# Fused attention and two feed-forward layers on one core: the first batch's last query tile moved behind the third unit, the third unit's gate products put ahead, values products tied behind later scores

## The chip, the core and the metric

The program runs on one core of a Trainium2 chip. The metric is the device time of one execution in microseconds (us). Engines by their short names: PE multiplies matrices (PEld is its weight load), DVE is the vector engine, ACT the scalar engine, POOL is GpSimd, and SP issues most of the DMAs. Every engine takes its instructions in the order in which the built program lists them.

## What is computed

```python
# attention: q, k, v (4, 8, 576, 64), block-causal mask with blocks of 64
scores = where(block_i >= block_j, q @ k.T / 8, -1e9)
x = softmax(scores) @ v                    # (4, 8, 576, 64) -> 2304 tokens x 512
# first layer: RMS norm, gate and values of width 1536
xn = x / sqrt(mean(x * x) + 1e-6) * rms_g
x = (silu(xn @ w_gate) * (xn @ w_val)) @ w_out
# second layer: one of 8 experts for every token
expert = argmax(cosine(x, expert_emb) / tau)
out = gate_w * (relu(x @ w1[expert]) @ w2[expert])
```

Products run in two half-precision parts (high and low), so that each takes three matrix products: high by high, high by low, low by high.

## The kernel before

**Tiles and units.** A batch has 576 tokens: four query tiles of 128 rows (t = 0 to 3) and a last one of 64 rows (t = 4). `TILES` lists the pairs (b, t) in the order in which attention is computed: for every batch tiles 0 and 1, then 2 and 3, then 4. The first layer works on nine units of 256 tokens: unit 0 is tiles (0,0) and (0,1), unit 1 is (0,2) and (0,3), unit 2 is (1,0) and (1,1), and so on; the four last tiles (b,4) together are unit 8. `need[u]` is the number of attention groups that must be done before unit u can start. A group is a few heads of one tile: all eight for t = 0, four for t = 1, two else.

**A group of attention.** `attend_a` loads and prepares the inputs that are due (`att_load`, `prep`: keys and queries are split and turned, for tiles from the fifth on by DMA transposes that SP issues), then computes the scores (`att_qk`, into two PSUM tiles `sc`, of which there are two), their maxima (`att_max`, on DVE and ACT), the exponentials (`att_exp`, ACT) and the split into high and low parts `ph` and `pl` (`att_split`; for t = 4 `pl` is made on DVE, L412, else on POOL, L417), which from the twelfth group on are turned by two DMA transposes into `pth` and `ptl`. `att_pv` multiplies these by the values into `av`. After a tile's last head, `fin_all` normalises it: x, jk, the power on POOL (L494), the scaling on DVE (L499), hl (ACT L505 and POOL L511), and a DMA transpose into the unit's columns `xT` (L513). `x` and `hl` have one buffer each.

**A unit of the first layer.** `gate_mm(u, s)` makes 24 gate and 24 values products for one of six slices of the width; `gate_t`, `gate_a` and `gate_b` make the two halves of `hT[s]` from them. `out_mm(u, j, s)` adds the slice to the output of token half j (six products a slice and half), and `out_ev` takes that output from PSUM to the tile `R` (one buffer), squares it in place (ACT L580, after which the PSUM tile `o` is free) and turns it (`x2T`).

**The order.** Three stages matter. In the list `pair`, four gates of unit 0 run between the groups of its neighbours; then 14 steps interleave the slices of unit 0's output with the gates of unit 1. Behind each step as many groups are attended as `want` says, up to `need[2] + AHEAD` at the end, and two weight steps (`w_step`: load, decode on DVE L189 to L193, split on ACT L203, L204 and POOL L205) follow. `tc.cur_priority` and a scheduler decide the final order there. From unit 2 on the PE order is written out by hand: `piece(u, s, n)` gives six pieces a slice (two of output of unit u - 1, then four of gates of unit u), and `due` says behind which piece the scores and the values products of each group come. Lines of the kernel after the change are two to twenty higher than before (L567 of the output products becomes L571, L530 becomes L535, L505 becomes L510, L411 and L412 become L413 and L414).

The table of inputs, `xt` (three buffers for the units' columns), `kv` (six for keys, seven for values) and the constants AHEAD = 3, LATER = 7 are the numbers that the change touches or relies on.

Of the kernel before, what the change touches and what calls it, by code (L numbers as in the profile page):

```python
# [18 lines left out]
P = 128  # L19
# [12 lines left out]
def attention_moe_moe(ctx: ExitStack, tc: tile.TileContext, q, k, v, w_gate, w_val, w_out, rms_g, emb, tau, w1, w2, out):  # L32
# [40 lines left out]
    xt_p = p1.enter_context(tc.tile_pool(name="xt", bufs=3))  # L73
    ps_s = p1.enter_context(tc.tile_pool(name="ps_s", bufs=2, space=PSUM))
    ps_a = p1.enter_context(tc.tile_pool(name="ps_a", bufs=1, space=PSUM))
    kv_p = p1.enter_context(tc.tile_pool(name="kv", bufs=6))
# [11 lines left out]
    AHEAD, NW0, NW1, NW2, WLAG, NLAG, LOADS, PREPS, PRI, EVERY, LATER = 3, 4, 2, 2, 2, 1, 3, 1, 300, 4.8, 7  # L88
# [205 lines left out]
    def prep_v(b, t):  # L294
        n = rows_of(t)
        vv = kv_p.tile([P, H, 2 * D], F16, tag="vT", name="vT", bufs=7)
        vT[b, t] = vv
        src = nat.pop(("v", b, t))[:n]
        nc.scalar.activation(out=vv[:n, :, 0:D], in_=src, func=ACTF.Copy, scale=QS)
        nc.gpsimd.tensor_tensor(out=vv[:n, :, D:2 * D], in0=src, in1=vv[:n, :, 0:D], op=ALU.subtract)  # L300
# [5 lines left out]
    sc_t = {}  # L306

    def att_qk(b, t, heads):
        scs = [ps_s.tile([P, 512], F32, tag="sc", name="sc") for _ in range(2)]
        sc_t[b, t, heads[0]] = scs  # L310
        if t < NTT - 1:
            keys = P * (t + 1)
            hpb = 512 // keys
            for bk, sc in enumerate(scs):
                for j, h in enumerate(heads[bk * hpb:(bk + 1) * hpb]):
# [5 lines left out]
                nc.tensor.matmul(  # L321
                    out=sc[:, 0:hpb * keys].rearrange("p (j k) -> p j k", k=keys)[:, :, keys - 64:keys],
                    lhsT=mask_l, rhs=mask_r[:, 0:64 * hpb].rearrange("p (j k) -> p j k", k=64),
                    start=False, stop=True, skip_group_check=True)
        else:
            half = S // 2
            for hf, sc in enumerate(scs):
# [5 lines left out]
                for c in range(2):  # L333
                    for n, (kt, a, z) in enumerate(pieces):
                        for j, h in enumerate(heads):
                            nc.tensor.matmul(out=sc[64 * j:64 * j + 64, a - hf * half:z - hf * half], lhsT=q_of(b, t, h, c),
                                             rhs=kT[b, kt][:, h, a - kt * P:z - kt * P],
                                             start=(c == 0 and n == 0), stop=(c == 1), skip_group_check=True)
# [95 lines left out]
    def att_pv(b, t, heads):  # L434
# [7 lines left out]
        for j, h in enumerate(heads):  # L442
            o = a[0][0:n, h, :]
            for kb in range(nkb):
# [6 lines left out]
                for i, (x, w) in enumerate(((lh, vv[0:kn, h, 0:D]), (lh, vv[0:kn, h, D:2 * D]), (ll, vv[0:kn, h, 0:D]))):  # L451
                    first = a[1] is None
                    mm = nc.tensor.matmul(out=o, lhsT=x, rhs=w, start=first, stop=(h == H - 1 and kb == nkb - 1 and i == 2), skip_group_check=True)  # L453
                    if first:
# [102 lines left out]
    fl = {}  # L557
# [313 lines left out]
    for u, (b, z) in enumerate(HALVES):  # L871
        TILES += [(b, 2 * z), (b, 2 * z + 1)]
        spot[b, 2 * z], spot[b, 2 * z + 1] = (u, 0), (u, P)
        if z:
            TILES.append((b, NTT - 1))
            spot[b, NTT - 1] = (NU - 1, b * (UNIT // B))
    groups = []
# [133 lines left out]
    n0, n1 = need[1], need[2] + AHEAD  # L1011
    for i, (kind, u, s, want) in enumerate(pair):
# [3 lines left out]
        while state["g"] < want:  # L1016
            attend()
            w_step(NW1 if i < 4 else 0)
# [14 lines left out]
    def piece(u, s, n):  # L1033
        if n < 2:
            out_mm(u - 1, n, s)
            if n and s == NFP - 1:
                out_ev(u - 1, 0)
                out_ev(u - 1, 1)
        else:
# [3 lines left out]
            if n == 5:  # L1043
                gate_a(u, s)
                gate_b(u, s)
# [3 lines left out]
                if s == 1:  # L1049
                    for f in (route_c, route_p, route_d):  # L1050
                        f(u - 2, [0, 1])

    with tc.manual_schedule(engines={ENG.PE}):
        for i in range(pieces + 1):
# [5 lines left out]
            if i < pieces:  # L1060
                piece(2 + i // (6 * NFP), i // 6 % NFP, i % 6)
# [198 lines left out]
```

## Time and profile before

| what | value |
|---|---|
| time, median of 3 runs | 867.86 us |
| time, lowest and highest | 864.2 and 868.99 us |
| the profiled execution's own time | 866.45 us |
| its span | 864.6 us |
| mean granted TensorE clock | 0.968 |
| busy: PE, DVE, ACT, POOL | 793.1, 464.2, 451.2, 355.3 us |

The span runs from the first to the last instruction; the time has 1.85 us more around it. The three runs lie within 0.6% of each other. PE is busy for 92% of the span, so the table alone says little: what the change can win is read from the stretch in which its order differs.

### The profile page before, as it was taken

To read this page: it belongs to the slowest core of one execution; us is meant where nothing else is said; L and a number is where in the kernel's file an instruction comes from. 1 tells how busy PE (TensorE), PEld (TensorE's weight loads), DVE (VectorE), ACT (ScalarE), POOL (GpSimd) and SP (SyncE) were. 2 spreads that over 40 slices of the span, in tenths; PEclk is the share of its full clock that TensorE was granted. 3 is DMA by queue.
4 is the path that set the end of the run, shared out by engine and by line. 5 is a ranking of instruction groups with operands and counts; after the bars stand their busy time and mean duration, and the time that the engine had idled before them with its cause. 6 is when DMAs were issued, how large, how long until landed. Compare 5 with 4: busy or idle time off the path is not lost. (4 is left out here: it accounts for less than half of the span.)

```text
span 864.6 us, 21945 instructions
## 1 busy us (share of the span) xinstructions
PE 793.1 (92%) x8590; PEld 602.7 (70%) x8590; DVE 464.2 (54%) x984; ACT 451.2 (52%) x929; POOL 355.3 (41%) x362
## 2 busy tenths in 40 slices
PE   3769799879999999989999999999899999999994
PEld 2669577657767777767777777767676777777771
DVE  6799988735255636245636254134573175471352
ACT  6888777755555656555656452122521274462352
POOL 5555556764552656542656521223314121202110
PEclk8789989999999999999999999999999999999998
DMA  8474799986688686587686351022784399897760
GB/s 243 145 193 140 165 244 232 158 155 107 111 162 156 105 135 124 112 157 152 114 135 119 77 106 32 7 49 50 218 247 113 77 300 302 216 316 197 185 154 22
DMA packets 291326, 130.39 MB, mean 151 GB/s; under 512 B 247613, under 2 KB 276456, under 8 KB 291211
## 3 DMA queue, kind: packets, MB, share of 16 engines
q1 hardware_dynamic: 283338, 112.28, 60.1%
q0 software_dynamic: 4080, 10.56, 4.3%
q10 hardware_dynamic: 3792, 6.03, 2.1%
q8 instruction: 70, 1.15, 0.6%
q14 instruction: 46, 0.37, 0.1%
HBM read 129.30 MB, written 10.25 MB: 161 GB/s over the span
## 5 line engine op out<-in xcount | busy, mean ns | idle before, releaser
L530 PE MATMUL g<-xT,wg 128*128 128x256 f16 x1296 | 157.0, 276 | 2.5 <-DMA xT<-hl 2.5
L567 PE MATMUL o<-wo,hT 128*128 128x512 f16 x648 | 153.5, 384 | 3.8 <-ACT o L580 3.8
L530 PE MATMUL v<-xT,wv 128*128 128x256 f16 x1296 | 156.7, 275 | 0.0
L530 PEld LDWEIGHTS <-wg 128*128 128x128 f16 x1296 | 125.9, 99 | 24.8 <-issue 1.8
L530 PEld LDWEIGHTS <-wv 128*128 128x128 f16 x1296 | 123.9, 98 | 15.4
L763 PE MATMUL h<-xt,whi 128*128 128x128 f16 x1280 | 109.8, 219 | 0.8 <-DVE xt L1073 0.8
L763 PE MATMUL h<-xt,wlo 128*128 128x128 f16 x640 | 108.4, 219 | 0.3 <-DVEq L736 0.3
L567 PEld LDWEIGHTS <-hT 128*128 128x128 f16 x648 | 60.7, 98 | 68.0 <-issue 6.3
L728 DVE SCALAR_TENSOR_TENSOR wlo<-raw,whi 128x1024 f16<-128x1024 f32 x64 | 77.6, 1239 | 46.2 <-ACT whi L727 44.2
L763 PEld LDWEIGHTS <-whi 128*128 128x128 f16 x1280 | 98.9, 98 | 5.0 <-issue 0.9
L787 PE MATMUL o<-whi,hl 128*128 128x512 f16 x320 | 96.4, 383 | 2.3 <-issue 2.3
L555 POOL TENSOR_TENSOR hT<-h,hT 128x512 f16<-128x512 f32 x54 | 63.2, 1170 | 70.3 <-ACT hT L554 68.4
L417 POOL TENSOR_TENSOR pl<-pf,ph 128x512 f16<-128x512 f32 x66 | 69.5, 1073 | 53.7 <-issue 46.7
L787 PEld LDWEIGHTS <-hl 128*128 128x128 f16 x480 | 46.3, 98 | 56.9 <-issue 5.9
L795 POOL DMA_INDIRECT out_dram<-ob,ido x18 | 21.0, 1168 | 151.4 <-ACTq L736 76.1
L727 ACT ACTIVATE whi<-raw 128x1024 f16<-128x1024 f32 x64 | 65.9, 1053 | 31.3 <-DMA raw<-in_moe_w_dram 19.9
L453 PE MATMUL av<-vT,ptl 128*128 128x64 f16 (+2 forms) x480 | 57.5, 198 | 25.5 <-DMA ptl<-pl 15.6
L353 DVE TENSOR_REDUCE nb<-sc 128x1 f32<-128x384 f32 (+3 forms) x88 | 54.0, 635 | 44.7 <-PE sc L321 44.4
L453 PE MATMUL av<-vT,pth 128*128 128x64 f16 (+2 forms) x960 | 65.7, 198 | 7.9 <-DVE c L193 3.5
L453 PEld LDWEIGHTS <-pth 128*128 128x128 f16 (+2 forms) x960 | 53.8, 105 | 19.3 <-DMA pth<-ph 9.1
L453 PEld LDWEIGHTS <-ptl 128*128 128x128 f16 (+2 forms) x480 | 45.9, 105 | 30.6 <-DMA ptl<-pl 18.5
L372 ACT ACTIVATE pf<-sc,nb 128x128 f32<-128x128 f32 (+3 forms) x128 | 65.9, 526 | 2.3 <-ACT nb L354 0.4
(230 smaller groups left out, 1300.4 us busy)
## 6 DMA issues: line engine op xcount, KB each, us to landing
raw<-in_moe_w_dram SPq DMA_DIRECT2D x172, 512.0 KB
st<-in_moe_w_out_dram SPq DMA_DIRECT2D x12, 512.0 KB
st<-in_moe_w_gate_dram SPq DMA_DIRECT2D x11, 512.0 KB
st<-in_moe_w_val_dram SPq DMA_DIRECT2D x11, 512.0 KB
x2s<-R ACTq DMA_DIRECT2D x18, 256.0 KB
nat<-in_k_dram SPq DMA_DIRECT2D x16, 256.0 KB
nat<-in_q_dram SPq DMA_DIRECT2D x16, 256.0 KB
nat<-in_v_dram SPq DMA_DIRECT2D x16, 256.0 KB
```

Of the source, the lines that this page charges most:

```text
L353: nc.vector.tensor_reduce(out=nb[:, z], in_=sc[:, 0:hpb * keys].rearrange("p (j k) -> p j k", k=keys), axis=AX.X, op=ALU.max)
L372: nc.scalar.activation(out=pf[:, j * keys:(j + 1) * keys], in_=scs[j // hpb][:, (j % hpb) * keys:(j % hpb + 1) * keys], func=ACTF.Exp, sca ...
L417: nc.gpsimd.tensor_tensor(out=pl[:, z:y], in0=pf[:, z:y], in1=ph[:, z:y], op=ALU.subtract)
L453: mm = nc.tensor.matmul(out=o, lhsT=x, rhs=w, start=first, stop=(h == H - 1 and kb == nkb - 1 and i == 2), skip_group_check=True)
L530: mm = nc.tensor.matmul(out=o[:, j, :], lhsT=w[cw][:, kt, f * P:(f + 1) * P], rhs=x[:, cx * KD + kt, :], start=(n == 0), stop=(n == 3 * KD ...
L555: nc.gpsimd.tensor_tensor(out=hT[1][fp], in0=h, in1=hT[0][fp], op=ALU.subtract)
L567: mm = nc.tensor.matmul(out=o, lhsT=hT[ch][f // 2][:, f % 2, j * P:(j + 1) * P], rhs=wo[cw][:, f, :], start=(f == 0 and n == 0), stop=(f = ...
L727: hi = nc.scalar.activation(out=whi[l][c], in_=raw[l][c], func=ACTF.Copy, scale=ES)
L728: lo = nc.vector.scalar_tensor_tensor(out=wlo[l][c], in0=raw[l][c], scalar=ES, in1=whi[l][c], op0=ALU.mult, op1=ALU.subtract)
L763: mm = nc.tensor.matmul(out=h[:, f, :], lhsT=w[:, kt, :], rhs=x[:, cx * KD + kt, :], start=(n == 0), stop=(n == 3 * KD - 1))
L787: nc.tensor.matmul(out=o, lhsT=x[:, cx, kt, :], rhs=w, start=(n == 0), stop=(n == 3 * K2 - 1))
L795: nc.gpsimd.indirect_dma_start(out=out, out_offset=bass.IndirectOffsetOnAxis(ap=(ido if ids is None else ids)[:, i:i + 1], axis=0), in_=ob ...
```

## The change

It has five parts. (1) Tile (0,4) is taken from the fifth place of `TILES` and put behind (1,1), so that its four groups come after those of unit 2's two tiles; `need[2]` falls from 18 to 14 and AHEAD rises from 3 to 7, which leaves the number of groups attended in the `pair` stage at 21. (2) In that stage, from the fifth step on, the values products of a group are written two groups later, and their first one is tied on PE behind the last score product written before it; the two that are left over go to the first two places of `due`. (3) For unit 2's first slice the four gate pieces come before the two output pieces of unit 1, and `gate_b` of that slice comes behind the output. (4) The units' columns have two buffers instead of three. (5) Keys have seven buffers instead of six, values eight instead of seven.

```diff
-    xt_p = p1.enter_context(tc.tile_pool(name="xt", bufs=3))
+    xt_p = p1.enter_context(tc.tile_pool(name="xt", bufs=2))
...
-    kv_p = p1.enter_context(tc.tile_pool(name="kv", bufs=6))
+    kv_p = p1.enter_context(tc.tile_pool(name="kv", bufs=7))
...
-    AHEAD, NW0, NW1, NW2, WLAG, NLAG, LOADS, PREPS, PRI, EVERY, LATER = 3, 4, 2, 2, 2, 1, 3, 1, 300, 4.8, 7
+    AHEAD, NW0, NW1, NW2, WLAG, NLAG, LOADS, PREPS, PRI, EVERY, LATER = 7, 4, 2, 2, 2, 1, 3, 1, 300, 4.8, 7
...
-        vv = kv_p.tile([P, H, 2 * D], F16, tag="vT", name="vT", bufs=7)
+        vv = kv_p.tile([P, H, 2 * D], F16, tag="vT", name="vT", bufs=8)
...
-    def att_pv(b, t, heads):
+    def att_pv(b, t, heads, behind=None):
...
+                    if behind:
+                        tc.add_manual_dep(mm.ins, behind, NOSYNC, reason="those scores go first")
+                        behind = None
...
+    TILES.insert(6, TILES.pop(4))
...
+    pend = []
     for i, (kind, u, s, want) in enumerate(pair):
...
         while state["g"] < want:
-            attend()
-            w_step(NW1 if i < 4 else 0)
+            if i < 4:
+                attend()
+                w_step(NW1)
+            else:
+                attend_a()
+                if len(pend) > 1:
+                    att_pv(*pend.pop(0), behind=fl['qk'])
+                pend.append(groups[state["g"] - 1])
...
     def piece(u, s, n):
         if n < 2:
             out_mm(u - 1, n, s)
+            if n and (u, s) == (2, 0):
+                gate_b(u, s)
...
-                gate_b(u, s)
+                if (u, s) != (2, 0):
+                    gate_b(u, s)
...
+    for g, a in zip((first - 2, first - 1), sorted(due)):
+        due[a].append(("pv", g))
...
-                piece(2 + i // (6 * NFP), i // 6 % NFP, i % 6)
+                piece(2 + i // (6 * NFP), i // 6 % NFP, i % 6 if i > 5 else (2, 3, 4, 5, 0, 1)[i])
```

In `att_qk` the score products also store their name in `fl['qk']`, and `fl = {}` moves up.

How the order of the built program moves is shown at three places. Names: `sc` are scores of a group, `kT` and `qT` turned keys and queries, `av` a tile's output, `o` the first layer's output of a token half, `g` and `v` gate and values products; a number behind a name tells buffers apart.

First place: PE, where the output of unit 0's first slices ends and unit 1's first gate (on xT_1181) begins. Before, with scores of tile (0,4) (sc_1878, sc_1992) and its values products (av_1764):

```order
L567 MATMUL o_1710<-wo1_194,hT0_1_196 128x512
...
L336 MATMUL sc_1878<-kT_242,qT_1595 64x128
...
L453 MATMUL av_1764<-vT_276,pth_1758 64x64
...
L336 MATMUL sc_1992<-kT_242,qT_1597 64x128
...
L453 MATMUL av_1764<-vT_276,ptl_1761 64x64
...
L567 MATMUL o_1703<-wo0_193,hT0_2_197 128x512
...
L530 MATMUL g_1815<-xT_1181,wg0_189 128x256
```

After, with scores of (1,1) in two groups (sc_1865, sc_1952), values products of (1,0) (av_1990), scores of (0,4) (sc_2180) and values products of (1,1) (av_2227):

```order
L571 MATMUL o_1716<-wo0_193,hT1_1_202 128x512
...
L320 MATMUL sc_1865<-kT_1734,qT_1738 128x128
...
L320 MATMUL sc_1952<-kT_1734,qT_1740 128x128
...
L455 MATMUL av_1990<-vT_1605,pth_1784 128x64
...
L571 MATMUL o_1709<-wo0_193,hT0_2_197 128x512
...
L338 MATMUL sc_2180<-kT_242,qT_1945 64x128
...
L455 MATMUL av_2227<-vT_1605,pth_1900 128x64
...
L535 MATMUL g_1808<-xT_1181,wg0_189 128x256
```

Four groups of scores now stand ahead of unit 1's first gate where three of (0,4) stood, and the first values products stand behind two later groups' scores.

Second place: ACT, up to the copy `hl` of tile (0,3), from which the second half of xT_1181 is turned. Before (`pf` are exponentials, `ph` high parts, `c` and the `w` names are weights):

```order
L378 ACTIVATE pf_1748,sums_1747<-sc_1717,nb_1743 128x288
L378 ACTIVATE pf_1748,sums_1747<-sc_1718,nb_1743 128x288
L203 ACTIVATE wv0_191<-c_1285 128x4x128
L204 ACTIVATE c_1285<-c_1285 128x512
L488 ACTIVATE jk_1674,fin_1670<-x_1669 128x512
L203 ACTIVATE wg0_189<-c_1425 128x4x128
L411 ACTIVATE ph_1754<-pf_1748,sums_1747 128x576
L204 ACTIVATE c_1425<-c_1425 128x512
L505 ACTIVATE hl_1679<-x_1669 128x512
```

After:

```order
L416 ACTIVATE ph_1779<-pf_1770 128x1024
L493 ACTIVATE jk_1680,fin_1676<-x_1675 128x512
L251 ACTIVATE qd_1937<-nat_1725 64x8x2x64
L204 ACTIVATE c_1425<-c_1425 128x512
L356 ACTIVATE nb_1885<-nb_1885 128x4
L203 ACTIVATE wv0_191<-c_1435 128x4x128
L374 ACTIVATE pf_1890,sums_1889<-sc_1865,nb_1885 128x256 x2
L374 ACTIVATE pf_1890,sums_1889<-sc_1866,nb_1885 128x256 x2
L204 ACTIVATE c_1435<-c_1435 128x512
L416 ACTIVATE ph_1895<-pf_1890 128x1024
L510 ACTIVATE hl_1685<-x_1675 128x512
```

Between the last group of (0,3) and this copy stood one group of (0,4); now a whole tile (1,0), the first group of (1,1) and the preparation of (0,4) stand there.

Third place: PE, where the output of unit 0 ends and that of unit 1 begins. Before (o_1710 is unit 0, o_3119 and o_3126 unit 1, g_3181 is unit 2's first gate on xT_2463):

```order
L567 MATMUL o_1710<-wo0_193,hT1_5_206 128x512
L530 MATMUL g_3060<-xT_1181,wg0_189 128x256
L567 MATMUL o_3119<-wo0_193,hT0_0_195 128x512
L530 MATMUL v_3085<-xT_1181,wv0_191 128x256
L567 MATMUL o_3126<-wo0_193,hT0_0_195 128x512
L530 MATMUL g_3181<-xT_2463,wg0_189 128x256
```

After (o_1716 is unit 0, o_3238 unit 1, g_3083 and v_3176 unit 2's first gate on xT_2028):

```order
L571 MATMUL o_1716<-wo0_193,hT1_5_206 128x512
L535 MATMUL g_3024<-xT_1181,wg0_189 128x256
L535 MATMUL v_3049<-xT_1181,wv0_191 128x256
L535 MATMUL g_3083<-xT_2028,wg0_189 128x256
L535 MATMUL v_3176<-xT_2028,wv0_191 128x256
L571 MATMUL o_3238<-wo0_193,hT0_0_195 128x512
```

Unit 1's output now waits for the PSUM tile of unit 0's behind 96 gate products. Outside these places the PE order is the same, row for row, up to the last groups of tile (0,3) and again from the second slice of unit 1's output on.

## Rows read from the trace of the kernel before

**Rows 1.** The page: busy time of each engine over the span.

```profile
PE 793.1 (92%) x8590; PEld 602.7 (70%) x8590; DVE 464.2 (54%) x984; ACT 451.2 (52%) x929; POOL 355.3 (41%) x362
```

**Rows 2.** Stretches: length, busy PE, PEld, DVE, ACT, POOL (instructions), granted clock, DMA share, GB/s.

```profile
93.10:111.83 18.73, 13.39 (x163) 8.27 (x162) 18.50 (x48) 13.79 (x33) 8.27 (x8) 0.84 0.68 184
111.83:204.30 92.47, 83.79 (x875) 65.80 (x874) 58.60 (x104) 62.04 (x145) 59.96 (x58) 0.92 0.98 189
```

**Rows 3.** Timeline of PE, where it stood idle: start, us, operation, [idle before, releaser].

```profile
105.75 0.32 PE L453 MATMUL av<-vT,pth 128*64 128x64 f16 x2 [3.48 <-DVE c L193]
...
111.83 4.77 PE L530 MATMUL g<-xT,wg 128*128 128x256 f16 x24 [1.07 <-DMA xT<-hl]
...
156.72 0.23 PE L453 MATMUL av<-vT,pth 128*128 128x64 f16 x2 [2.53 <-DMA pth<-ph]
...
192.63 2.72 PE L567 MATMUL o<-wo,hT 128*128 128x512 f16 x6 [3.09 <-ACT o L580]
```

**Rows 4.** Timeline of PE, at full clock: what products take from start to start.

```profile
119.43 0.74 PE L336 MATMUL sc<-kT,qT 128*64 128x128 f16 x24
...
123.15 0.22 PE L453 MATMUL av<-vT,ptl 128*64 128x64 f16 x1
...
124.67 0.94 PE L530 MATMUL v<-xT,wv 128*128 128x256 f16 x7
...
143.90 3.19 PE L567 MATMUL o<-wo,hT 128*128 128x512 f16 x14
146.93 2.78 PE L530 MATMUL g<-xT,wg 128*128 128x256 f16 x24
...
161.37 2.78 PE L530 MATMUL g<-xT,wg 128*128 128x256 f16 x24
163.99 2.56 PE L530 MATMUL v<-xT,wv 128*128 128x256 f16 x22
166.39 0.50 PE L318 MATMUL sc<-kT,qT 128*128 128x128 f16 x6
...
167.12 0.38 PE L530 MATMUL v<-xT,wv 128*128 128x256 f16 x2
...
172.92 0.22 PE L453 MATMUL av<-vT,pth 128*128 128x64 f16 x2
...
173.62 0.22 PE L453 MATMUL av<-vT,pth 128*128 128x64 f16 x2
```

**Rows 5.** Timeline of ACT: prices, and the copies of tile (0,3).

```profile
83.14 0.62 ACT L505 ACTIVATE hl<-x 128x512 f16<-128x512 f32 x1
83.66 0.62 ACT L203 ACTIVATE wo<-c 128x512 f16<-128x512 f32 x1
...
93.80 0.60 ACT L397 ACTIVATE pth<-pT 128x512 f16<-128x512 f32 x1
...
103.40 0.63 ACT L505 ACTIVATE hl<-x 128x512 f16<-128x512 f32 x1 [0.31 <-DVE x L499]
...
140.47 0.36 ACT L372 ACTIVATE pf<-sc,nb 128x128 f32<-128x128 f32 x1
...
145.61 1.08 ACT L414 ACTIVATE ph<-pf 128x1024 f16<-128x1024 f32 x1
...
157.94 0.47 ACT L372 ACTIVATE pf<-sc,nb 128x256 f32<-128x256 f32 x1
```

**Rows 6.** Timeline of SP: the transpose of tile (0,3) into xT.

```profile
106.98 1.23 SPq L513 DMA_TRANSPOSE xT<-hl  x1
```

**Rows 7.** Timeline of POOL: first and last of six instructions without a gap.

```profile
147.88 2.27 POOL L417 TENSOR_TENSOR pl<-pf,ph 128x512 f16<-128x512 f32 x2
...
153.44 1.16 POOL L555 TENSOR_TENSOR hT<-h,hT 128x512 f16<-128x512 f32 x1
```

**Rows 8.** Timeline of DVE: the scaling of a tile, twice.

```profile
102.62 0.74 DVE L499 SCALAR_TENSOR_TENSOR x<-x,fin,g_b 128x512 f32<-128x512 f32 x1
...
148.38 6.76 DVE L499 SCALAR_TENSOR_TENSOR x<-x,fin,g_b 64x512 f32<-64x512 f32 x1
```

More of the change, by code (lines that the diff above doesn't have):

```diff
@@ L306, in attention_moe_moe @@
     sc_t = {}
+    fl = {}
     def att_qk(b, t, heads):
@@ L320, in att_qk @@
                                              skip_group_check=True)
-                nc.tensor.matmul(
+                fl['qk'] = nc.tensor.matmul(
                     out=sc[:, 0:hpb * keys].rearrange("p (j k) -> p j k", k=keys)[:, :, keys - 64:keys],
                     lhsT=mask_l, rhs=mask_r[:, 0:64 * hpb].rearrange("p (j k) -> p j k", k=64),
-                    start=False, stop=True, skip_group_check=True)
+                    start=False, stop=True, skip_group_check=True).ins.name
         else:
@@ L335, in att_qk @@
                         for j, h in enumerate(heads):
-                            nc.tensor.matmul(out=sc[64 * j:64 * j + 64, a - hf * half:z - hf * half], lhsT=q_of(b, t, h, c),
+                            fl['qk'] = nc.tensor.matmul(out=sc[64 * j:64 * j + 64, a - hf * half:z - hf * half], lhsT=q_of(b, t, h, c),
                                              rhs=kT[b, kt][:, h, a - kt * P:z - kt * P],
-                                             start=(c == 0 and n == 0), stop=(c == 1), skip_group_check=True)
+                                             start=(c == 0 and n == 0), stop=(c == 1), skip_group_check=True).ins.name
     pt_t = {}
@@ L555, in gate_b @@
         nc.gpsimd.tensor_tensor(out=hT[1][fp], in0=h, in1=hT[0][fp], op=ALU.subtract)
-    fl = {}
     x2T = {}
```

## The prediction, made before the changed kernel was run

> **What bounds the kernel now.** I read the page first: PE is busy 793.1 of 864.6 us [rows 1], so a change that adds no work can win only from PE's idle time and from stretches at the lower clock. The order shows where to look: PE's products differ only between the last group of tile (0,3), at 93.1 us, and the second slice of unit 1's output, at 204.3 us. The second view is therefore the table of stretches [rows 2]. From 93.10 to 204.30, 111.2 us, PE is busy 97.2 and idle 14.0, and the granted clock is 0.84 and 0.92. The third view, PE's timeline, names the idle places: 3.48 us before the first values product of (0,4), 1.07 before unit 1's first gate, 2.53 before those of (1,0), 3.09 where unit 1's output waits for ACT to free the PSUM tile of unit 0's [rows 3]. After such a pause PE runs at the lower clock: 24 gate products took 4.77 us at 111.83 and 2.78 at 146.93 [rows 3, 4].
>
> The products of this stretch can be priced at full clock [rows 4]. Gates and values: 2.62 us for 24, 0.109 each. Output: 3.03 for 14, 0.216 each. Scores: 0.74 a group of (0,4), else 0.73 for 14, 0.052 each. Values products: 0.70 for 24, 0.029 each, and for (0,4) 1.52 for 29, 0.052 each. The stretch holds 432 gates (47.2), 84 output products (18.2), four score groups of (0,4) and 128 other score products (3.0 + 6.7), 150 values products and 120 of (0,4) (4.4 + 6.3), and about 1.5 of small ones: 87.3 us. So 24 us is the most that any order could win, 14 of idle time and 10 of low clock.
>
> **The change part by part.**
>
> *Tile (0,4) later, tied values products: the first half.* The stretch to unit 1's first gate is one in which DVE is busy 18.50 of 18.73 us [rows 2]. The change takes the four groups of (0,4), whose low parts DVE makes, out of it and puts in (1,0) and (1,1), whose low parts POOL makes. DVE is relieved; ACT, in order and filled, becomes the engine that ends last. Its list tells when unit 1's second half of columns can be ready. The first `pth` copy of (0,3)'s last group started at 93.80 [rows 5]; now one 1024-wide copy stands ahead of it, 1.08 long and about 0.98 from start to start, so 94.8. From there to the copy `hl` of (0,3) stand 15 instructions of 512 columns, 0.52 from start to start (7.8), two more 1024-wide ones and the third, `ph` of (1,1) (2.9), eight exponentials of 128 columns at 0.36 (2.9), four of 256 at 0.47 (1.9) and two small ones (0.4) [rows 5]: 15.9 us, so `hl` starts at 110.7 instead of 103.40. From there to the gate it took 8.43 us before, with the transpose issued at 106.98 [rows 3, 5, 6]. POOL now has the low part of (1,1), 2.27 us [rows 7], ahead of `hl`'s, which begins at 110.7 too and costs 1.65 beyond the copy's own 0.62. So unit 1's first gate starts at 110.7 + 8.4 + 1.6 = 120.7 us instead of 111.83: the first half is 8.9 us **later**. PE will stand idle there, mostly at the first values products of (1,0) (whose transposes cannot be issued before ACT's `ph`) and at the scores behind them, which need one of two `sc` tiles back.
>
> *The second half.* What is left from that gate to the end of the stretch is 432 gates (47.2), 52 output products (11.2), three groups of (0,4) scores (2.2), 74 other score products (3.9), 100 values products (2.9), 120 of (0,4) (6.3), router (0.5): 74.2 us, where it took 92.47. I add 2.0 for the low clock behind the pause, as at 111.83. The waits: every group's values products now stand behind a later group's scores, so that the transposes have a gate's time more; the 2.53 us at 156.72 should go.
>
> *Gates of unit 2 ahead of unit 1's output.* 96 gate products (10.5), scores (0.7) and 18 values products (0.5), 11.7 us, now stand between the last output product of unit 0 and the first of unit 1. Before, the first half of unit 1's output stood right behind, and the second half came 3.09 us too early for its tile [rows 3]. Against the change: both halves of unit 0 now end together, so the second must pass the one tile `R` behind the first, its transpose (about 4.9 us, the 106.98 to 111.83 of [rows 3, 6]) included, and the copies; 11.7 covers that with little to spare, and I leave half a microsecond of the 3.09 in the waits below. The low clock behind that wait (2.72 us for six products, where 0.216 each would be 1.3 [rows 3, 4]) goes too.
>
> *Two buffers for columns.* Unit 2's columns now take the buffer of unit 0, so SP's transpose of (1,0) waits for unit 0's last gate, and everything behind it on SP's list with it: the transposes of (1,2) first. `x` and `hl` have one buffer, so (1,1), then (0,4) follow: a transpose of 4.9 us again and a chain of about as much, against 13.4 us of PE work (66 gates 7.2, 58 values products of (0,4) 3.0, 28 scores 1.5, eight output products 1.7) before PE needs (1,2)'s output tile. I cost it at nothing; if that cover is short it shows as a wait of `av`. More key and value buffers, and the two values groups moved into `due`, cost nothing: no product is added.
>
> *Sum.* For the waits that stay in the second half I take 2.0 us of the 8.7 idle before (92.47 less 83.79 [rows 2]). The stretch ends at 120.7 + 2.0 + 74.2 + 2.0 = 198.9 instead of 204.3. That is 5.4 us less than the profiled execution's own 866.45 (which lies 1.4 below the median of the three runs, 867.86): **861.0 us**. Bounds of the uncertain terms: the gate at 111.83, if ACT's list keeps its old pace, or at 126.7, if the chain is hit by one such block as at 148.38 (below, 6.0 us); waits of 0 to 5 in the second half. That is 850 to 870.
>
> **A rule against it.** At 148.38 DVE's scaling of a tile took 6.76 us, at 102.62 it took 0.74 [rows 8]. In the first case POOL worked through six instructions without a gap from 147.88 to 154.60 and DVE ended half a microsecond after the last [rows 7]; it was held through all six. The change fills POOL's list in just the place where the scaling of (0,3) falls. On the row's price a hit there that nothing hides adds 6.0 us to the sum: 867. The Trainium skill ("SBUF — State Buffer", section "Who interferes with whom") says that a DVE instruction with two SBUF inputs contends with a GpSimd instruction that reads SBUF and that the one that issues first holds the port for the whole instruction; read as one instruction of waiting, 1.16 us at most, its price would make the sum 861 to 862 even with such a hit. The row shows longer.
>
> **Rivals.**
> (a) *The wait only moves.* The first gate starts later still, at 123 to 126, since SP's list puts three weight loads ahead of that transpose, each waiting for DVE to free a buffer. For it: DVE at 99% in the first half. Against it: DVE loses the work of (0,4) there. The second half's gain is then spent: gain -1 to 3.5, 863 to 867, say 865.5.
> (b) *The first half costs nothing.* DVE was its only limit, ACT keeps up, and the gate comes at 112 to 114: gain 12 to 14, 853. Against it: the ACT sum above, which has no idle time in it.
> (c) *Slower: DVE is held by POOL.* POOL's runs in the first half and after hold the scaling of (0,3), (1,0) and (1,1) and the low parts of (0,4) as at 148.38. One hit of 6.0 is mostly hidden behind the ACT chain; two more, in front of DVE's steps on gate products, stop PE, 12.0 less 5.4: 6.6 slower, 873. It decides from about 10 us of holding on. For it: one such row; against it: POOL must have no gap in its run, and at 102.62 the same step took 0.74 [rows 8].
> That the ties are not kept is ruled out by the order, which shows them on PE.
>
> **How the numbers follow.** About 0.5% (4.3 us) can be told from no change. My forecast, a gain of 2 to 9 us, has 0.48 (0.34 beyond 4.3, 0.14 within), (a) 0.20 (all within), (b) 0.18 (beyond), (c) 0.14 (0.12 slower, 0.02 within). Faster 0.52, same 0.36, slower 0.12. The range of 853 to 868.5 leaves out (c) and the best part of (b).
>
> **What would show it.** Right: PE idle by more than before ahead of unit 1's first gate, which starts at about 120; no wait of some 3 us at unit 1's first output; hardly any idle time and a clock of 1.00 from there to the router; everything behind the stretch only shifted. Wrong: the gate before 115 or after 125; a DVE row of several us in the stretch; PE waiting for `av` after unit 0's last gate; a difference behind the second slice of unit 1's output.

## The result, and the profile after

The changed kernel takes 861.4 us (median of 8 runs, 857.1 to 861.92) against 868.08 of 8 runs of the kernel before: ratio 0.9914, 95% interval 0.989 to 0.9938 (the two medians alone give 0.9923). In a second set, on another chip, it was 0.9925 (0.9895 to 0.9954). It is faster by 0.75 to 0.86%, 6.5 to 7.5 us; 861.0 was predicted. The profiled execution took 859.82 us, with a span of 858.0.

The page has the same totals as before [rows 1], to within 6 us:

```profile
PE 787.3 (92%) x8590; PEld 600.6 (70%) x8590; DVE 464.2 (54%) x984; ACT 449.7 (52%) x929; POOL 355.1 (41%) x362
```

The table of stretches (columns as in [rows 2]) is cut at the same three places of the program as there: the last group of tile (0,3), unit 1's first gate, the second slice of unit 1's output.

```profile
92.48:122.58 30.10, 18.10 (x169) 11.29 (x170) 26.14 (x39) 23.29 (x64) 22.03 (x20) 0.79 1.10 228
122.58:201.97 79.39, 76.95 (x869) 61.96 (x868) 53.69 (x121) 51.28 (x113) 44.79 (x44) 1.00 0.78 160
201.97:858.00 656.03, 628.14 (x6804) 470.17 (x6800) 305.97 (x657) 300.30 (x579) 235.59 (x230) 0.99 0.64 142
```

The first part takes 30.10 us where it took 18.73, and PE is busy in it for 18.10 us instead of 13.39. The second takes 79.39 instead of 92.47, at a clock of 1.00 instead of 0.92, with 2.4 us idle instead of 8.7. Little of this is work that changed its place. Counted by kind and priced by [rows 4], an estimate, the first part's products come to about 11.9 us against 10.2 before, so 1.8 us moved ahead of the gate (six more output products are 1.3 of it); the rest of the 4.7 us by which PE is busier there goes with the low clock (0.79; an output product took 441 ns on average, before 398). Over both parts PE idles 14.4 us instead of 14.0 and is busy for 95.05 instead of 97.18: the change put the idle time ahead of the gate, and what is behind it then runs at full clock. So the stretch ends at 201.97 instead of 204.30: 2.33 us, not 5.4. The other 4.27 us of difference in span lie behind it, where the program is the same (before, the last part took 864.60 - 204.30 = 660.30). That needs an explanation, below.

PE's timeline in the first part and at the end of the second (start, us, operation, [idle before, releaser]):

```profile
109.45 0.82 PE L320 MATMUL sc<-kT,qT 128*128 128x128 f16 x8 [4.47 <-ACT pf L374]
112.59 0.23 PE L455 MATMUL av<-vT,ptl 128*128 128x64 f16 x1 [1.00 <-DMA ptl<-pl]
118.07 1.23 PE L338 MATMUL sc<-kT,qT 128*64 128x128 f16 x24 [3.27 <-DMA qT<-qd]
122.50 0.26 PE L455 MATMUL av<-vT,pth 128*128 128x64 f16 x2 [0.53 <-DVE x L484]
122.58 3.16 PE L535 MATMUL g<-xT,wg 128*128 128x256 f16 x24
...
197.69 0.18 PE L612 MATMUL L<-enT,x2T 128*128 128x16 f16 x1 [0.62 <-DMA x2T<-R]
...
197.91 2.75 PE L571 MATMUL o<-wo,hT 128*128 128x512 f16 x12
```

PE idles at scores that wait for an `sc` tile and at the scores of (0,4), whose turned queries are late. The gate itself runs almost at full clock (3.16 us for 24, where [rows 3] show 4.77). Unit 1's output now runs without the 3.09 us wait of [rows 3].

The chain that sets the gate, on ACT, POOL and SP (three timelines):

```profile
95.16 1.06 ACT L251 ACTIVATE qd<-nat 128x1024 f16<-128x1024 f32 x1 [2.06 <-DMA qT<-qd]
96.12 0.58 ACT L399 ACTIVATE pth<-pT 128x512 f16<-128x512 f32 x1
...
110.69 1.08 ACT L416 ACTIVATE ph<-pf 128x1024 f16<-128x1024 f32 x1
111.64 0.66 ACT L510 ACTIVATE hl<-x 128x512 f16<-128x512 f32 x1
...
123.44 0.63 ACT L203 ACTIVATE wg<-c 128x512 f16<-128x512 f32 x1 [5.45 <-DVE c L193]
```

```profile
112.19 1.15 POOL L205 TENSOR_TENSOR wv<-c,wv 128x512 f16<-128x512 f32 x1
113.32 2.26 POOL L419 TENSOR_TENSOR pl<-pf,ph 128x512 f16<-128x512 f32 x2
115.55 1.15 POOL L516 TENSOR_TENSOR hl<-x,hl 128x512 f16<-128x512 f32 x1
```

```profile
116.97 1.24 SPq L518 DMA_TRANSPOSE xT<-hl  x1
```

`hl` of (0,3) starts at 111.64 (predicted 110.7), its low part waits on POOL behind a weight's and (1,1)'s low part until 115.55, and the transpose is issued at 116.97 instead of 106.98 [rows 6]. The last release ahead of the gate is another one: the values products at 122.50 wait 0.53 us for an `av` tile from DVE.

DVE was held for long once, as the rule against the change had it, but in a tiny instruction of 128x8:

```profile
109.58 1.64 DVE L504 SCALAR_TENSOR_TENSOR x<-x,fin,g_b 128x512 f32<-128x512 f32 x1 [0.59 <-POOL fin L499]
...
115.90 5.27 DVE L482 TENSOR_SCALAR fin<-sums 128x8 f32<-128x8 f32 x1
```

It ends at 121.17, when POOL, without a gap until then, is through with a weight's low part (119.99 + 1.15). ACT's 5.45 us of idle time behind it is its shadow.

### The profile page after: what moved, and what is told of

It reads as the page before. It is cut to its first block, busy times and chain, and to the rows that moved or that the text cites. A ratio compares the mean times of both kernels' runs of the same rounds, so it can differ in the third digit from the quotient of the medians.

```text
span 858.0 us, 21966 instructions
## 1 busy us (share of the span) xinstructions
PE 787.3 (92%) x8590; PEld 600.6 (70%) x8590; DVE 464.2 (54%) x984; ACT 449.7 (52%) x929; POOL 355.1 (41%) x362
## 3 DMA queue, kind: packets, MB, share of 16 engines
q8 instruction: 70, 1.15, 0.6%
## 5 line engine op out<-in xcount | busy, mean ns | idle before, releaser
L535 PE MATMUL g<-xT,wg 128*128 128x256 f16 x1296 | 154.9, 273 | 1.4 <-DVE t L552 0.9
L571 PE MATMUL o<-wo,hT 128*128 128x512 f16 x648 | 151.5, 382 | 0.0
L767 PEld LDWEIGHTS <-wlo 128*128 128x128 f16 x640 | 62.6, 98 | 1.4 <-DVE wlo L732 0.8
```

The lines of the kernel that those rows point to most:

```text
L535: mm = nc.tensor.matmul(out=o[:, j, :], lhsT=w[cw][:, kt, f * P:(f + 1) * P], rhs=x[:, cx * KD + kt, :], start=(n == 0), stop=(n == 3 * KD ...
L571: mm = nc.tensor.matmul(out=o, lhsT=hT[ch][f // 2][:, f % 2, j * P:(j + 1) * P], rhs=wo[cw][:, f, :], start=(f == 0 and n == 0), stop=(f = ...
L767: mm = nc.tensor.matmul(out=h[:, f, :], lhsT=w[:, kt, :], rhs=x[:, cx * KD + kt, :], start=(n == 0), stop=(n == 3 * KD - 1))
```

## Experiments

**The theory** after this reading: the idle time stands ahead of unit 1's first gate, with a little more PE work in it, and behind the gate no product stands before its transpose, so that PE keeps its clock there; the parts need each other. **The rivals:** one part is the gain by itself (tile, gates, buffers); the gain lies behind the stretch, where 4.27 us appeared; DVE's hold is what limits it.

To compare executions I cut each at four marks: the last PE transposes of (0,3), unit 1's first gate, the first router product (`L`) of unit 0 and that of unit 1. Sum 1 is the distance from the first mark to the last, us; the tail runs from there to the end, in code that all share but for the buffers and, in e11 and e12, the places of the values products. Ratios are to the kernel before on the same chip.

| kernel | ratio (95%) | to the gate | to router 0 | to router 1 | sum 1 | tail |
|---|---|---|---|---|---|---|
| before | 1 | 17.74 | 91.11 | 66.08 | 174.9 | 595.6 |
| changed | 0.9914 (0.989 to 0.9938) | 29.05 | 74.15 | 69.80 | 173.0 | 591.5 |
| changed again (e5) | 0.9925 (0.9895 to 0.9954) | 28.94 | 72.05 | 68.31 | 169.3 | 601.2 |
| e1 gates ahead alone | 1.0058 (1.003 to 1.0086) | 17.80 | 92.74 | 68.62 | 179.2 | 597.7 |
| e2 tile and buffers alone | 1.0065 (1.0035 to 1.0095) | 30.75 | 90.01 | 66.19 | 187.0 | 596.5 |
| e3 no gates ahead | 0.9972 (0.9943 to 1.0002) | - | - | - | - | - |
| e4 no delay | 1.0066 (1.0037 to 1.0096) | 28.89 | 80.73 | 72.80 | 182.4 | 593.5 |
| e6 no hold | 0.9917 (0.9889 to 0.9945) | 28.66 | 71.73 | 70.19 | 170.6 | 599.8 |
| e7 ramp later | 1.0031 (0.9998 to 1.0064) | 23.42 | 81.83 | 73.40 | 178.7 | 600.9 |
| e8 buffers alone | 0.9974 (0.9941 to 1.0007) | 17.77 | 90.69 | 66.06 | 174.5 | 601.7 |
| e9 weights later | 1.0025 (0.9997 to 1.0053) | 22.83 | 80.31 | 70.26 | 173.4 | 601.3 |
| e10 the same, three steps | 1.0139 (1.0102 to 1.0177) | 23.18 | 84.55 | 79.44 | 187.2 | 596.8 |
| e11 values later, 8 | 0.9917 (0.9884 to 0.995) | 29.24 | 72.01 | 70.11 | 171.4 | 594.4 |
| e12 values later, 9 | 0.9919 (0.9885 to 0.9952) | 28.96 | 74.04 | 68.59 | 171.6 | 597.0 |

The profiled execution of e3 took 880.58 us, the longest of its twelve (median 866.97), so only a wait is read from it. Router 0 is not the same place in both orders of the pieces; the gate, router 1 and the end are.

**e1, gates ahead alone**, in the kernel before:

```diff
         out_mm(u - 1, n, s)
+        if n and (u, s) == (2, 0):
+            gate_b(u, s)
...
-                gate_b(u, s)
+                if (u, s) != (2, 0):
+                    gate_b(u, s)
...
-                piece(2 + i // (6 * NFP), i // 6 % NFP, i % 6)
+                piece(2 + i // (6 * NFP), i // 6 % NFP, i % 6 if i > 5 else (2, 3, 4, 5, 0, 1)[i])
```

> The kernel before with part 3 alone: unit 2's first four gate pieces ahead of unit 1's first output. My theory (each part pays only because of the others): in the old order the second transpose of unit 2's columns is issued only at 191.7 us, so PE, done with unit 1's gates at about 189.5, now stands before the gate for some 7 us, until about 196.5, where it stood 3.1 us before the output; the wait for the output's PSUM tile goes. Sum: 2 to 4 us slower than before, about 871. Rival (the gates ahead are the gain by themselves): the 3.1 us wait and the 1.4 us of low clock behind it go, 4 to 5 us faster, about 864. What lies behind the second slice of unit 1's output takes the 660.3 us of before by my theory.

Measured: 0.58% slower, about 5 us. PE's timeline:

```profile
191.08 0.29 PE L453 MATMUL av<-vT,pth 128*128 128x64 f16 x2 [2.10 <-DMA pth<-ph]
...
196.22 4.41 PE L530 MATMUL g<-xT,wg 128*128 128x256 f16 x24 [2.37 <-DMA xT<-hl]
```

The gate starts at 196.22, about where it was expected (196.5); the wait for `o` is gone, and the waits for `pth`, `ptl` and `xT` ahead of it take its place. The gates ahead are no gain where unit 2's columns come this late.

**e2, tile and buffers alone** (parts 1, 4 and 5 in the kernel before; the lines are those of the change).

> The kernel before with parts 1, 4 and 5 (tile moved, buffers), without the delayed values products and without the gates ahead. My theory: the first half comes later, as in the changed kernel (unit 1's first gate at 120 to 123 us), the second half wins back the waits for pth, the wait of about 3 us at unit 1's first output stays: 0 to 5 us slower than before, 868 to 873. Rival (moving the tile is the gain; DVE is relieved): 3 to 6 us faster, 862 to 865. Second rival (the larger buffers are the gain, behind the stretch): the time from unit 1's second output slice to the end falls from 660.3 to about 656 us, whatever the stretch does.

Measured: 0.65% slower, about 5.7 us; the tile's move is no gain by itself. The first part is nearly that of the changed kernel (30.75 against 29.05 and 28.94), and the waits of the second are all there, the last of them at unit 1's output:

```profile
127.50 0.23 PE L453 MATMUL av<-vT,pth 128*128 128x64 f16 x2 [1.78 <-DMA pth<-ph]
134.48 0.25 PE L453 MATMUL av<-vT,pth 128*64 128x64 f16 x2 [1.29 <-DMA pth<-ph]
...
202.97 2.72 PE L567 MATMUL o<-wo,hT 128*128 128x512 f16 x6 [2.67 <-ACT o L580]
```

**e3, the changed kernel without the gates ahead** (e1's lines taken back).

> The changed kernel without part 3: unit 2's first slice in the usual order of pieces. My theory: the wait for the output's PSUM tile comes back, about 3 us, with about 1.5 us of low clock behind it: 3 to 5 us slower than the changed kernel, 864.5 to 866.5. Rival (the gain is in the tile and the delay): within 1 us of the changed kernel, 861 to 862.

Measured: 0.9972, so about 4 to 5 us slower than the changed kernel's 0.9914 and 0.9925, as expected. The wait is back:

```profile
196.99 1.48 PE L571 MATMUL o<-wo,hT 128*128 128x512 f16 x6 [2.84 <-ACT o L584]
```

**e4, the changed kernel without the delay:**

```diff
-            if i < 4:
-                attend()
-                w_step(NW1)
-            else:
-                attend_a()
-                if len(pend) > 1:
-                    att_pv(*pend.pop(0), behind=fl['qk'])
-                pend.append(groups[state["g"] - 1])
+            attend()
+            w_step(NW1 if i < 4 else 0)
...
-    for g, a in zip((first - 2, first - 1), sorted(due)):
-        due[a].append(("pv", g))
```

> The changed kernel without part 2: every group's values products are written right behind its scores, no tie. My theory: values products stand on PE before their transposes have landed, waits for pth and ptl of 2 to 3 us each come back at two or three places in unit 1's stretch: 2 to 5 us slower than the changed kernel, 863.5 to 866.5. Rival (the delay costs as much in the first half as it gives): within 1 us of the changed kernel, or up to 3 us faster, 858 to 862.5.

Measured: 1.0066, some 12 to 13 us slower than the changed kernel, where I expected 2 to 5. The gate comes at the same distance (28.89), and all of the loss lies behind it:

```profile
126.03 0.23 PE L455 MATMUL av<-vT,pth 128*128 128x64 f16 x2 [2.56 <-DMA pth<-ph]
132.68 0.25 PE L455 MATMUL av<-vT,pth 128*64 128x64 f16 x2 [0.97 <-DMA pth<-ph]
...
194.49 0.23 PE L455 MATMUL av<-vT,pth 128*128 128x64 f16 x2 [3.18 <-DMA pth<-ph]
203.83 0.19 PE L612 MATMUL L<-enT,x2T 128*128 128x16 f16 x1 [2.45 <-DMA x2T<-R]
```

Of the delay, the tie itself does little: without it the built PE order differs in the place of two products only, so it was not run apart.

**e5, the changed kernel again.**

> The changed kernel once more, unaltered, on the chip of the three runs below. My theory: the 4.3 us by which the part behind the stretch was shorter in the profiled execution than in that of before is not the change's, since the runs so far show the same code behind unit 1's router take 591.5 to 597.7 us in different executions: this time the part from unit 1's router (its first product) to the end is as likely above 594 as below, and the time against before stays at 0.986 to 0.995. Rival (larger buffers, or two buffers for columns, shorten what lies behind): again 590 to 592.5 us from that router to the end.

Measured: 0.9925, and a tail of 601.2 us where the first execution had 591.5. The stretch table of this execution (same three cuts):

```profile
93.98:123.97 29.99, 18.64 (x169) 11.32 (x169) 26.59 (x44) 24.58 (x67) 22.93 (x21) 0.77 1.08 226
123.97:201.15 77.18, 76.45 (x866) 61.73 (x866) 51.25 (x118) 50.68 (x111) 44.19 (x45) 1.00 0.82 166
201.15:865.50 664.35, 630.79 (x6804) 470.20 (x6800) 305.34 (x654) 299.74 (x578) 235.02 (x230) 0.99 0.63 140
```

The stretch takes 107.17 us here, 109.49 in the first execution, 111.20 before; what lies behind takes 664.35, more than before's 660.30. The 4.27 us behind the stretch were not the change's.

**e6, no hold:** the tensor_scalar of L482 becomes a reduction over an axis of length one; all engines keep their order.

```diff
-            nc.vector.tensor_scalar(out=st[:n, 0:H], in0=sm[:n, 0:H], scalar1=1e-9, scalar2=QS, op0=ALU.add, op1=ALU.mult)
+            nc.vector.tensor_reduce(out=st[:n, 0:H], in_=sm[:n, 0:H].unsqueeze(2), axis=AX.X, op=ALU.add)
```

> The changed kernel in which the small step on the sums (128x8, ahead of a tile's normalisation) is a reduction over an axis of length one on DVE instead of a tensor_scalar; the term 1e-9, far below the last bit of sums that are at least 1, is left out. The order of all engines is the same. At 115.90 the tensor_scalar took 5.27 us, until POOL's run ended. My theory: the reduction isn't held (about 0.2 us), but PE waits for unit 1's columns until about 122 anyway, so the first gate comes 0 to 1 us earlier, ACT's idle 5.45 us behind it goes, and the whole is 0 to 2 us faster than the changed kernel. Rival (the hold is what makes the first half late): the first gate comes 3 to 5 us earlier, the whole 3 to 5 us faster. Second rival: the reduction, or the reciprocal behind it, is held as long.

The instruction on DVE, first in e5 (the changed kernel's second execution), then here:

```profile
117.26 1.94 DVE L482 TENSOR_SCALAR fin<-sums 128x8 f32<-128x8 f32 x1
```

```profile
117.69 0.15 DVE L482 TENSOR_REDUCE fin<-sums 128x8 f32<-128x8 f32 x1
```

The reduction is not held, in the middle of a POOL run without a gap (117.33 to 122.9). The time stays: 0.9917. The gate is 28.66 us behind the first mark against 28.94 and 29.05, so it hardly depends on the hold. Behind the gate the long hold shows all the same. The two profiled executions that have it (the first, and e12 with 5.28 us) take 74.15 and 74.04 us from the gate to router 0; e5 and e11, with 1.94 and 1.69, take 72.05 and 72.01, and e6 71.73. The difference is two waits of PE, which only those two have, 0.88 and 0.94 us in the first execution (130.70, 138.07), and in e12:

```profile
128.47 0.20 PE L455 MATMUL av<-vT,ptl 128*128 128x64 f16 x1 [0.67 <-DMA ptl<-pl]
...
135.93 2.78 PE L535 MATMUL g<-xT,wg 128*128 128x256 f16 x24 [1.03 <-DVE t L552]
```

The DVE step of the second wait (L552) starts 14.8 us behind the gate in the first execution (137.34) and 12.0 in e5 (135.95). So a long hold goes with about 2 us; that it causes them is the likely reading and no run of its own shows it, since e5, beside which e6 was timed, had a short one in its profile. The Trainium skill ("SBUF — State Buffer", section "Who interferes with whom") says that a tensor_scalar can take the port pair that GpSimd shares and that a tensor_reduce on this chip never does: the two rows of L482 agree.

**e7, ramp one step later:**

```diff
-            want = n0 + -(-(n1 - n0) * (i - 3) // (len(pair) - 4))
+            want = n0 + max(0, -(-(n1 - n0) * (i - 4) // (len(pair) - 5)))
```

> The changed kernel with the groups of the pair stage attended one step later (the ramp of want begins one step later and ends at the same number). Three groups stand ahead of unit 1's first gate instead of four; ACT's list up to hl of (0,3) loses the preparation of (0,4) and the second ph (about 3.5 us), POOL's list some 5 us. My theory (the first half is bound by ACT's and POOL's lists up to hl): hl at 107 to 109, the first gate at 114 to 117 instead of 122.6, and since the second half is nearly all PE work, most of that stays: 3 to 6 us faster than the changed kernel. Rival (work only moves behind the gate, and tile (0,4)'s columns or transposes become late there): within 1.5 us of the changed kernel, or slower.

Measured: the gate comes where I expected it, at 115.85, and the kernel is about 1.1% slower than the changed one. Its stretches by the four marks, and three rows of PE:

```profile
92.43:115.85 23.42, 13.83 (x126) 8.12 (x124) 18.90 (x37) 19.94 (x57) 14.53 (x13) 0.80 1.01 221
115.85:197.68 81.83, 77.08 (x834) 62.45 (x835) 48.65 (x108) 49.50 (x106) 46.42 (x44) 0.93 0.86 163
197.68:271.08 73.40, 66.22 (x756) 49.61 (x753) 32.73 (x89) 39.15 (x86) 35.59 (x35) 0.98 0.70 132
```

```profile
132.75 0.73 PE L338 MATMUL sc<-kT,qT 128*64 128x128 f16 x24 [2.02 <-DMA qT<-qd]
...
159.79 0.22 PE L455 MATMUL av<-vT,pth 128*64 128x64 f16 x2 [2.51 <-DVE ph L424]
...
201.45 0.18 PE L612 MATMUL L<-enT,x2T 128*128 128x16 f16 x1 [3.43 <-DMA x2T<-R]
```

The gate is 5.6 us nearer than in the changed kernel (23.42 against 28.94 and 29.05), but PE has been busy for only 13.83 us ahead of it, where the changed kernel, cut in the same way, has 17.05 and, in e5, 17.60. What is left behind the gate comes with waits of its own: 4.8 and 7.2 us idle in the two stretches behind (81.83 - 77.08, 73.40 - 66.22), against 0.2 and 3.6 in e5. By the prices of [rows 4] only about 2.1 us of products moved behind the gate (six output products and a group of (0,4)'s scores), so most of the loss is in these waits and in the lower clock (0.93 and 0.98). An early gate is not what the first part is worth.

**e8, buffers alone** (parts 4 and 5 in the kernel before).

> The kernel before with parts 4 and 5 alone (two buffers for columns, seven for keys, eight for values); the order of PE is that of before. My theory: no product needs them in the old order: within 2 us of before, the part from unit 1's router to the end within the 591 to 598 of the other runs. Rival (buffers are part of the gain): 3 to 5 us faster than before, that part at 590 to 592.5. Second rival: two buffers for columns hold up the transposes of unit 2 in the old order: 1 to 4 us slower.

Measured: 0.9974, an interval that holds 1, and a sum 1 of 174.5 against 174.9. The two buffers for columns cost nothing that can be told, the larger ones for keys and values give nothing that can be told.

**e9 and e10, weights later:** in the constants of the changed kernel NW1 is 1 instead of 2; in e10 NW2 is also 3 instead of 2.

```diff
-    AHEAD, NW0, NW1, NW2, WLAG, NLAG, LOADS, PREPS, PRI, EVERY, LATER = 7, 4, 2, 2, 2, 1, 3, 1, 300, 4.8, 7
+    AHEAD, NW0, NW1, NW2, WLAG, NLAG, LOADS, PREPS, PRI, EVERY, LATER = 7, 4, 1, 2, 2, 1, 3, 1, 300, 4.8, 7
```

> The changed kernel with NW1 = 1: one weight step (decode on DVE, two copies on ACT, one subtraction on POOL) behind each of the eight groups attended with unit 0's first gates, where it is two; the eight steps come behind the later steps of the list, still ahead of what needs them. All four engines keep their work; the same tiles are attended. On ACT the copy hl of (0,3) now stands ahead of the exponentials and the ph of (1,1) and of two weight copies (1.9 + 0.95 + 1.0 = 3.9 us), on POOL hl's low part ahead of (1,1)'s low part and a weight's (3.4 us). My theory (the first half ends when ACT's and POOL's lists let the transpose of (0,3) go, 29 us behind the last PE transpose of (0,3) in two executions of the changed kernel): that distance falls to 23 to 26 us, some 2.4 us of PE work (part of unit 0's output, half of the scores of (0,4)) moves behind the gate, and the whole is 1 to 4 us faster than the changed kernel. Rival (as in the run with the later ramp, what moves behind the gate loses its cover and the second half gives everything back): within 1 us of the changed kernel or slower.

> As the run before it, with three weight steps instead of two behind each later step of the list (NW2 = 3), so that the weights are done at the same place as in the changed kernel. My theory: the first gate as in the run before, the second half more crowded on DVE and ACT in its first 20 us: 0 to 3 us faster than the changed kernel. Rival: the crowding brings waits back, slower than the run before by 2 us or more.

Measured: 1.0025 and 1.0139, so about 1 and 2% slower than the changed kernel, a clear miss. The gate came 22.83 and 23.18 us behind the first mark, as forecast, so the chain over ACT and POOL was read rightly and its worth wrongly: as in e7, PE has been busy for only 13.3 and 13.9 us by then, and the way from gate to router 0 grows to 80 and 85 us. In e10 the output of unit 0 then reaches the router far too late:

```profile
211.33 0.20 PE L612 MATMUL L<-enT,x2T 128*128 128x16 f16 x1 [8.37 <-DMA x2T<-R]
```

In e9 sum 1 is only 0.4 us above the first execution of the changed kernel; and its first mark, 96.01, is 1 to 2.5 us later. Against e5 it loses 4.1 us in sum 1, 1.0 ahead of the first mark and nothing in the tail; where the rest of its 9 us lies the one profile doesn't show.

**e11 and e12, values later from unit 2 on** (LATER 8 and 9 instead of 7 in the changed kernel), as a try for a version better than both.

> The changed kernel with LATER = 8: from unit 2 on, the values products of a group come eight pieces behind its scores instead of seven, which is what the delay in the pair stage does for unit 1. Behind the stretch the changed kernel's PE waits 11 to 14 us in all for ptl, mostly 0.5 to 2 us at a time. My theory (those waits are like the ones that the delay took out of unit 1's stretch): one piece more, 1.3 us of PE work, takes most of them: 4 to 8 us faster than the changed kernel, the part from unit 1's router to the end at 588 to 594. Rival (with two buffers of pth and ptl, a transpose must wait for the values products two groups back, which now come later, so the wait stays): within 2 us of the changed kernel.

> The same with LATER = 9. My theory: 0 to 2 us faster than the run with 8. Rival (the buffers): scores come every 4.8 pieces, so the transpose two groups on has 0.6 pieces left before its buffer is wanted: its wait comes back and the run is 1 to 6 us slower than the run with 8.

Measured: 0.9917 (0.9884 to 0.995) and 0.9919 (0.9885 to 0.9952), the same as the changed kernel, so the theory of e11, 4 to 8 us faster, missed. Groups of PE from 200 to 530 us (busy us, mean ns | idle before us), first e5, then e12:

```profile
L571 PE MATMUL o<-wo,hT 128*128 128x512 f16 x372 | 88.2, 383 | 1.0 <-ACT o L584 1.0
...
L455 PE MATMUL av<-vT,ptl 128*128 128x64 f16 (+1 forms) x314 | 35.8, 194 | 13.1 <-DMA ptl<-pl 13.1
```

```profile
L571 PE MATMUL o<-wo,hT 128*128 128x512 f16 x384 | 89.8, 379 | 7.4 <-ACT o L584 7.4
...
L455 PE MATMUL av<-vT,ptl 128*128 128x64 f16 (+1 forms) x319 | 36.6, 194 | 5.9 <-DMA ptl<-pl 5.9
```

The wait for `ptl` falls from 13.1 to 5.9 us, and one for `o` rises from 1.0 to 7.4: the wait changes its place. In e11 `ptl` has 7.1, `o` 1.0, and the wait for `pth` rises from 0.6 to 3.0. No version here beats the changed kernel.

## Why the prediction was right, point by point

**The time** was right (861.0 against 861.4) and so was the sign of each half, but that the number is so close is partly luck. The forecast took 5.4 us from an execution of 866.45 that lies 1.6 below the median of 868.08; the median gained 6.7. In the sum several errors cancel, below, and where the last microseconds of the median lie the profiles don't show. Two of the signs that were to show it wrong came, a DVE row of several us and a difference behind the second slice; the first cost little and the second went away in e5.

**First half.** Predicted: the gate at 120.7, 8.9 us later than before. Measured: 122.58, and by the marks 29.0 us behind the last transposes of (0,3) instead of 17.74; e5 and e6 agree to 0.4. The chain named was the right one and its length was right: ACT takes 15.5 us from that `pth` (96.12) to `hl` (111.64), where 15.9 was worked out. What failed is its start: I put `pth` at 94.8, but ACT stood idle for 2.06 us ahead of `qd`, for a buffer that a transpose of queries frees. POOL's extra 1.6 us was sized well (from `hl` to the transpose 5.33 us, before 3.58). From the transpose to the gate it took 5.6 us instead of 4.85, the last half for the values products ahead of the gate, whose `av` tile DVE freed late, behind its hold; in e5 it is 5.2 (118.73 to 123.97). The 2.0 us for low clock behind the pause were too much: the gate's 24 products took 3.16 us once and 2.78 in e5 and e6.

**Second half.** Predicted 78.2 us from the gate to the second slice (74.2 + 2.0 + 2.0); measured 79.39 and, in e5, 77.18. The sum holds, its terms do not: PE is busy for 76.95 and 76.45 us where the work term says 74.2, the 2.0 for low clock came to 0.4 and nothing, and the waits took 2.4 and 0.7 instead of 2.0. Most of the missing work is in a place that a sum of prices does not see: the built order puts seven score products of (0,4) singly between `v` products of the first layer, which the order before does nowhere in the stretch. In e12, and alike in both executions of the changed kernel:

```profile
140.74 0.23 PE L338 MATMUL sc<-kT,qT 128*64 128x96 f16 x1
140.90 0.28 PE L535 MATMUL v<-xT,wv 128*128 128x256 f16 x1
141.11 0.23 PE L338 MATMUL sc<-kT,qT 128*64 128x96 f16 x1
```

A pair takes 0.37 us from start to start, where the prices of [rows 4] give 0.14; the seven (140.74 to 143.36) cost about 1.6 us more. No run keeps this group of scores together. By the stretch the gain is 1.7 us (111.20 to 109.49) in the first execution and 4.0 in e5, against a forecast of 5.4: 2.1 us less busy time in both, and 0.4 us more idle time in the first, 1.9 less in e5. The median gained 6.7 and 7.5.

**The gates ahead** were priced at the 3.09 us wait and 1.4 of low clock behind it. e3 measures 4 to 5. The half microsecond that was to stay is there, 0.62 us at 197.69 and 0.50 in e5. The price holds only with the other parts: alone they lose 5 us (e1), and without the delay they gain nothing (e2 against e4, 1.0065 and 1.0066).

**The delay** was priced at the 2.53 us wait at 156.72. That is the step that was too small: it is worth 8 us without the gates ahead (e2 1.0065, e3 0.9972) and 12 to 13 with them (e4 1.0066). I counted the wait that stood in the old order; the new order without the delay has its own, 2.56, 0.97 and 3.18 us at (1,1)'s and (0,4)'s products, and 2.45 at the router.

**The tile's move** I took as the part that frees DVE. With the buffers alone it loses about 5.7 us (e2). What it brings to the whole is in part argued: about 1.8 us of products stand ahead of the gate that stood behind it, and (0,4)'s products, which stood at the waits of the first part, stand where PE has none.

**Two buffers** for columns: the waits for `av` behind unit 0's last gate are the 0.53 us above and one of 0.22 in e5, both for DVE, and e8 is the same as before. Three buffers in the changed kernel were not tried; memory has no room for them beside the larger keys and values.

**Rival (c)**, the hold: it came (5.27 us), in an instruction that the prediction had not named, and it goes with about 2 us behind the gate (e6), where the prediction had 6.0 for a hit that nothing hides. Ahead of the gate nearly all of it is hidden, as the prediction said of a single hit, because PE waits there for (0,3)'s transpose. **Rival (b)** falls with the gate at 122.58. **Rival (a)**, a gate at 123 to 126, is what e5 and e6 nearly show (123.97, 123.60 in their own time, of which 1.5 us is a later start), but the gain is not spent by it. The weight loads on SP's list held the transpose up little: POOL's low part of `hl` ended at 116.70 (in e5 at 118.06), the transpose was issued at 116.97 (118.73), with one load in between. **Everything behind only shifted** holds within the spread of executions: the tails in the table lie from 591.5 to 601.7 without an order by kernel.

**Open:** the stretch shows 1.9 to 5.6 us by sum 1 (174.9 less 173.0 and 169.3), the medians 6.7 and 7.5. The three runs that change little in the stretch, e6, e11 and e12, show 170.6, 171.4 and 171.6, and e8, like before, 174.5; so about 3.5 us of sum 1 are the change's by the means of five and two executions. With tails that differ by 10 us, the rest can't be placed.

## What to carry to other kernels

The end of one wait is not its price. Three runs brought the gate 5.5 to 6.2 us forward, and all were slower by 1% or more than the kernel that they changed: in e7 the two stretches behind it idled for 12.0 us, where e5 had 3.8. Ask where the idle time goes, and whether the engine keeps its clock there. Price a part of a combined change by the waits of the new order without it, not by those of the old order. And a difference of 4 us behind the place of the change is not yet a finding: run the same kernel once more.

## What the runs showed of the hardware

How long DVE is held by POOL differs between executions of one program: the same 128x8 tensor_scalar, in the same POOL run, took 5.27 us once and 1.94 the next time, and 0.17 at 102.84, where POOL was idle. In e4 and e12 it took 5.27 and 5.28, in e11 1.69. The scaling of (0,3), beside POOL, took 1.64, 1.62 and 1.64 us in three executions where it took 0.74 before [rows 8], and POOL's own weight step beside it took 1.60 instead of 1.15 each time, so that both sides pay:

```profile
110.63 1.60 POOL L205 TENSOR_TENSOR wg<-c,wg 128x512 f16<-128x512 f32 x1
```

The Trainium skill ("SBUF — State Buffer", "Who interferes with whom") gives the shared ports to whoever issues first, for the whole of its instruction. In the first execution the wait was longer than any one POOL instruction of the run (1.60 us at most): there the measurement decides.
